# Attention, soft MoE and MLP in one kernel: another order of the attention turns, earlier preparation of two pairs, five more pooled chunks on GpSimd

## The chip, the cores and the metric

The kernel runs on one NeuronCore of one Trainium2 chip. The metric is the device time of one execution in microseconds (us). Before the change the median of 3 runs is 683.52 us (681.71 to 686.23).

## The reference, cut to what matters

Three layers run one after the other, all in float32:

```
k_p, v_p = mean over each 8 neighbouring rows of k, v      # 576 -> 72 rows
scores = q @ k_p.T / sqrt(64);  attn = softmax(scores);  x = attn @ v_p     # 8 batches x 8 heads
logits = x @ phi                                            # 4608 tokens, 32 slots
slot_in = softmax over tokens(logits).T @ x                 # dispatch
slot_out[e] = relu(slot_in[e] @ w1[e]) @ w2[e]              # 8 experts, w1 512x1024, w2 1024x512
y = softmax over slots(logits) @ slot_out                   # combine
out = (s * relu(y @ w_in)**2 + b) @ w_out                   # 512 -> 2048 -> 512
```

## The kernel before, in words

**The attention loop** (L709) is where the change lies. The 4608 tokens are 36 tiles of 128 queries. The 8 batches form four pairs (pr 0 to 3) of 9 tiles each; the first tile of a pair mixes the leftover 64 queries of both its batches. The loop has 38 turns, and it is a software pipeline written out by hand: turn t works on tile t in stage A, on tile t-2 in stage B, and so on. The stages and the engines that they use are:

- **A** (L348): four transposes of q on TensorE (L360) into a PSUM bank, one copy out by ScalarE (L362). After tiles 4 and 8 of a pair (counted from 0) it gives a q buffer back, so a load can be issued.
- **B**, tile t-2 (L372): scores on TensorE (L390) into one of two `sc` PSUM tiles; VectorE takes the row maximum `mx` (L397) and subtracts it into `S` (L399). There are two `S` buffers, so B of one tile writes the buffer that the tile two before it used.
- **C**, tile t-3 (L401): exp on ScalarE (L407), row sums `sm` and the reciprocal `rs` on VectorE (L408, L411), and the product P = S * rs on GpSimd (L428). This product is the last reader of the `S` buffer.
- **D**, tile t-5 (L436): five transposes of P on TensorE (L441, L442) into two banks, two copies by ScalarE (L447, L448).
- **E**, tile t-6 (L454): logits on TensorE (L464, L471), one copy by ScalarE. **F**, tile t-7 (L478): two transposes (L487) and a reduction by VectorE (L489). E and F do work in five of nine turns.
- **r** advances the running dispatch of a batch by one step (L540): small chains of TensorE, VectorE and ScalarE that end in the matmuls of L584 to L628. Its step with the transpose at L551 needs `md` from VectorE (L544).
- **p** advances the preparation of the next pair by one step (L637). A pair has six chunks, three of k and three of v. A chunk is pooled by three additions in SBUF (L258, L262, L263; the first `next` issues L258, the second the other two and gives the chunk's buffer back). In a plan, `kd2` means the next part of k chunk 2 on VectorE, `vg0` the next part of v chunk 0 on GpSimd, `K2` or `V2` the three transposes of that chunk on TensorE (L273) with their copies on ScalarE. After nine such steps come v_prep2, v_prep3 and v_prep1.

The order of the letters in LOOP (for turn t, the string t mod 9) or FIRST (turns 2 to 9) is the program order on every engine, and every engine works strictly in that order. PREP names the turns in which the preparations of pairs 1, 2 and 3 begin; PLAN1 is the plan of pair 1, PLAN2 that of pairs 2 and 3. The four-bank pool `w` holds the results of A, D, E, F and r in turn, so TensorE also waits where an earlier bank has not been read.

**Loads.** All loads are issued by SyncE (SP), in one fixed list: k, q and v of the pairs, then 32 expert weights of 1 MB, then the MLP's weights. There are 8 ring and 3 raw buffers of 1 MB; a load is issued when a buffer has been given back (`done`, L144). At the end of turn 32 the preparation's buffers become four more (`x`), and after the loop more come free as the attention's pools close (the X steps of TAIL).

**After the loop** come a tail of remaining steps (TAIL, L771), the expert layers in the order of their weights (L978), and the MLP, 576 x 3 matmuls of 512 columns at L1148. None of these is touched.

Of the kernel before, what the change touches and what calls it, by code (L numbers as in the profile page):

```python
# [25 lines left out]
CUT = 1  # L26

LOOP = (
# [9 lines left out]
)  # L38
FIRST = {
# [8 lines left out]
}  # L48
PREP = (5, 11, 19)
PLAN1 = "kd0 kd0|K0 kg1|kg1|K1 kd2 kd2 vg0|K2 vg0|vg2 vd1 V0 vg2 vd1||V1 V2"  # L50
PLAN2 = "kd2 kg0|kd2 kg0|kg1 K2|kg1 K0|vg0 vd2|vd2 vg0|V2 vg1 K1|V0 vg1|V1"
NRING, NRAW = 8, 3
LTB = 1
XR = (4, 2, 2, 2)
# [5 lines left out]
def kernel(  # L60
# [576 lines left out]
    def prep(pr):  # L637


        plan_ = PLAN1 if pr == 1 else PLAN2  # L640
        plan_ = [st.split() for st in plan_.split("|")]
        eng = {op[0] + op[2]: nc.gpsimd if op[1] == "g" else nc.vector for st in plan_ for op in st if len(op) == 3}
        ch = {(nm, c): pool_chunk(nm, pr, c, eng[f"{nm}{c}"]) for nm in "kv" for c in range(3)}
        for st in plan_:
            for op in st:
                if op[0] in "kv":
                    next(ch[op[0], int(op[2])], None)
                else:
                    kv_transpose(op[0].lower(), pr, int(op[1]))
            yield  # L650
        v_prep2(pr)
        yield
        v_prep3(pr)
        yield
        v_prep1(pr)
# [12 lines left out]
    def first_v():  # L668
        def pool_v(c, eng):
            for _ in pool_chunk("v", 0, c, eng):  # L670
                pass

        pool_v(0, nc.gpsimd)
        yield
        pool_v(1, nc.vector)
        pool_v(2, nc.gpsimd)
        yield
        kv_transpose("v", 0, 0)
        kv_transpose("v", 0, 1)
        yield  # L680
        kv_transpose("v", 0, 2)
        v_prep2(0)
        yield
        v_prep3(0)
        yield
        v_prep1(0)
# [15 lines left out]
    def advance(gens):  # L702
        for g in list(gens):
            if next(g, gens) is gens:
                gens.remove(g)
# [3 lines left out]
    for t in range(NT + 2):  # L709
        for op in (FIRST.get(t) or LOOP[t % 9]).split():  # L710
# [22 lines left out]
            elif op == "p":  # L733
                if t == 2 and not preps:
                    preps.append(first_v())
                if t in PREP:
                    preps.append(prep(PREP.index(t) + 1))
                advance(preps)
# [551 lines left out]
```

## Time and profile before

| what | value |
|---|---|
| median of 3 runs | 683.52 us |
| profiled execution, its own time | 682.68 us |
| span of its instructions | 680.9 us |
| busy: PE, DVE, ACT, POOL | 647.3, 470.2, 410.6, 288.3 us |
| mean granted clock of TensorE | 0.986 |

The profile names the engines PE (TensorE matmuls), PEld (its weight loads), DVE (VectorE), ACT (ScalarE), POOL (GpSimd) and SP (SyncE). L390 is line 390 of the kernel. Busy times overlap between engines. A granted clock of 1.00 is TensorE at its upper level of 2.4 GHz, 0.5 at its lower level of 1.2 GHz. Times within the trace count from the span's start; about 1.8 us of the execution lie outside the span.

### The profile page before, as it was taken

How to read it: one execution, taken by the hardware profiler on the slowest of the kernel's cores; microseconds unless marked ns; L12 is line 12 of the kernel's file. 1: busy time of each engine (PE TensorE's matmuls, PEld its weight loads, DVE VectorE, ACT ScalarE, POOL GpSimd, SP SyncE). 2: the span in 40 equal slices, each digit the busy share in tenths (PEclk: the TensorE clock that was granted, in tenths of full speed). 3: DMA queues.
4: the chain of work that ended last, by engine and by line, in shares of the span. 5: the costliest groups of instructions: out<-in, count | busy, mean ns of one | idle time of the engine just before them, and what ended most of it. 6: DMA issues, size and time to landing. Idle time of an engine off the chain costs nothing.

```text
span 680.9 us, 11539 instructions
## 1 busy us (share of the span) xinstructions
PE 647.3 (95%) x4474; PEld 523.7 (77%) x4474; DVE 470.2 (69%) x753; ACT 410.6 (60%) x684; POOL 288.3 (42%) x222
## 2 busy tenths in 40 slices
PE   7777999899899999999999999999999999999996
PEld 6666777678664678888888888888888888888885
DVE  4779678667775687887765978887557754566443
ACT  3564677566425578875666666666666666555551
POOL 3766567522211444462314433463233241999100
PEclk9897999999998999999999999999999999999999
DMA  8999476609699911110111110310100000222222
GB/s 291 403 341 280 175 247 250 231 20 317 256 333 375 389 63 63 62 28 36 63 63 33 46 46 1 124 62 4 60 0 1 1 0 1 93 93 93 93 93 92
DMA packets 41318, 88.88 MB, mean 131 GB/s; under 512 B 6960, under 2 KB 15152, under 8 KB 41264
## 3 DMA queue, kind: packets, MB, share of 16 engines
q1 hardware_dynamic: 41264, 88.16, 37.1%
q8 instruction: 35, 0.57, 0.4%
q14 instruction: 19, 0.16, 0.1%
HBM read 78.71 MB, written 9.44 MB: 129 GB/s over the span
## 4 chain that ended last, share of the span: by engine, by line
PE 80%; DVE 9%; DMA 5%; ACT 4%; issue 1%; SPq 1%; DVEq 0%; ACTq 0%
PE o L1148 58%; PE h L1088 5%; DMA ring<-in_moe_w_dram 3%; PE sc L390 3%; DVE sm L408 2%; DVE S L399 2%; DVE mx L397 1%; PE w L441 1%; PE w L607 1%; PE w L360 1%; DMA ring<-in_q_dram 1%; ACT S L407 1%; PE so_ps L998 1%; PE w L584 1%; PE w L250 1%
## 5 line engine op out<-in xcount | busy, mean ns | idle before, releaser
L1148 PE MATMUL o<-whi,gh 128*128 128x512 f32 x576 | 225.3, 391 | 0.6 <-DVE gh L1074 0.6
L1148 PE MATMUL o<-wlo,gh 128*128 128x512 f32 x576 | 224.9, 391 | 0.0
L1148 PE MATMUL o<-whi,gl 128*128 128x512 f32 x576 | 209.4, 392 | 0.0
L1116 DVE TENSOR_TENSOR gl<-r,gh 128x768 fp32r<-128x768 f32 (+1 forms) x97 | 105.8, 1092 | 115.2 <-ACT gh L1108 114.0
L1100 ACT ACTIVATE r<-h 128x768 f32<-128x768 f32 x94 | 76.5, 814 | 141.2 <-PE h L1088 139.2
L1148 PEld LDWEIGHTS o<-whi,gl 128*128 128x128 f32 x576 | 108.1, 188 | 23.2 <-DVE gl L1116 0.5
L1148 PEld LDWEIGHTS o<-whi,gh 128*128 128x128 f32 x576 | 108.1, 188 | 21.1 <-issue 1.0
L1148 PEld LDWEIGHTS o<-wlo,gh 128*128 128x128 f32 x576 | 108.2, 188 | 18.9
L842 POOL TENSOR_TENSOR fr<-fr,xp 128x512 f32<-128x512 f32 x28 | 45.3, 1616 | 176.9 <-ACT fr L841 156.5
L1161 DVE SCALAR_TENSOR_TENSOR part<-o,sb_t,part 128x512 f32<-128x512 f32 x144 | 96.9, 740 | 3.2 <-PE o L1148 3.1
L1101 ACT ACTIVATE r<-r 128x768 f32<-128x768 f32 x94 | 79.7, 848 | 3.0
L1108 ACT CAST gh<-r 128x768 fp32r<-128x768 f32 x94 | 78.6, 836 | 2.6
L428 POOL TENSOR_TENSOR P<-S,rs 128x576 f32<-128x576 f32 x32 | 37.3, 1166 | 69.9 <-DVE rs L411 36.5
L1259 POOL TENSOR_TENSOR part<-part,wsum 128x512 f32<-128x512 f32 x36 | 53.3, 1519 | 15.1 <-ACT wsum L1253 15.1
L1088 PE MATMUL h<-cT,S 128*128 128x384 f32 x192 | 49.5, 338 | 0.0
L1088 PEld LDWEIGHTS h<-cT,S 128*128 128x128 f32 x192 | 36.0, 188 | 8.1
L408 DVE TENSOR_REDUCE sm<-S 128x8 f32<-128x584 f32 x36 | 27.3, 758 | 21.1 <-ACT S L407 21.0
L390 PE MATMUL sc<-kb,qT 128*128 128x144 f32 x256 | 39.7, 301 | 0.2 <-ACT qT L362 0.2
L397 DVE TENSOR_REDUCE mx<-sc 128x8 f32<-128x576 f32 x36 | 26.4, 734 | 15.9 <-PE sc L390 13.2
L390 PEld LDWEIGHTS sc<-kb,qT 128*128 128x128 f32 x256 | 35.8, 203 | 0.7 <-ACT qT L362 0.5
L407 ACT ACTIVATE S<-S 128x576 f32<-128x576 f32 x36 | 24.7, 686 | 18.6 <-DVE S L399 17.5
L362 ACT COPY qT<-w 128x512 f32<-128x512 f32 x36 | 20.9, 584 | 21.3 <-PE w L360 20.4
(247 smaller groups left out, 901.1 us busy)
## 6 DMA issues: line engine op xcount, KB each, us to landing
x<-in_moe_w_dram SPq DMA_DIRECT2D x14, 1024.0 KB, 9.7
ring<-in_moe_w_dram SPq DMA_DIRECT2D x12, 1024.0 KB, 7.5
raw<-in_moe_w_in_dram SPq DMA_DIRECT2D x8, 1024.0 KB, 5.6
raw<-in_moe_w_out_dram SPq DMA_DIRECT2D x8, 1024.0 KB, 5.0
out_dram<-part SPq DMA_DIRECT2D x32, 256.0 KB, 2.6
ring<-in_q_dram SPq DMA_DIRECT2D x7, 1024.0 KB, 10.9
ring<-in_v_dram SPq DMA_DIRECT2D x9, 768.0 KB, 11.6
ring<-in_k_dram SPq DMA_DIRECT2D x7, 768.0 KB, 7.5
```

The costliest lines, as they stand in the source:

```text
L390: nc.tensor.matmul(out=sc[:, i // 2, 2 * KP * (i % 2):2 * KP * (i % 2) + 2 * KP], lhsT=qT[:, i, :], rhs=kb[:, H * bb + 4 * (j % 2) + i, :] ...
L408: nc.vector.tensor_reduce(out=sm, in_=S, axis=AX.X, op=ALU.add)
L428: nc.gpsimd.tensor_tensor(out=o, in0=S, in1=rb, op=ALU.mult)
L842: nc.gpsimd.tensor_tensor(out=fr, in0=fr, in1=xp, op=ALU.mult)
L1088: nc.tensor.matmul(out=h[x][:, 0:384] if i == 0 else h[:, x, 0:384], lhsT=Sw[:, f, :], rhs=cT(c, 384), start=True, stop=True)
L1100: nc.scalar.activation(out=r, in_=h[:, :, 0:384], func=ACTF.Relu)
L1101: nc.scalar.activation(out=r, in_=r, func=ACTF.Square)
L1108: nc.scalar.copy(out=gh_t[i], in_=r)
L1116: nc.vector.tensor_tensor(out=gl[:, x], in0=r[:, x], in1=gh[:, x].bitcast(F32), op=ALU.subtract)
L1148: nc.tensor.matmul(out=o_t[tt], lhsT=l[:, x, 128 * c:128 * c + 128], rhs=r, start=(fi == 0 and n == 0), stop=(fi == GROUPS[g] - 1 and n == 1),
L1161: nc.vector.scalar_tensor_tensor(out=p, in0=o_t[tt], scalar=sb_t[:, 0:1], in1=p, op0=ALU.mult, op1=ALU.add)
L1259: nc.gpsimd.tensor_tensor(out=p, in0=p, in1=wsum, op=ALU.add)
```

## The change

It writes the letters of every turn in another order, starts the preparations of pairs 1 and 2 one turn earlier, and rewrites both plans. In PLAN1, k chunk 0 moves from VectorE to GpSimd; k chunk 2 and v chunk 1 stay on VectorE. In PLAN2, which runs twice, k chunk 2 and v chunk 2 move to GpSimd, so that all six chunks are there. Some turns now have two p or none, and three or more r or none. The instructions are otherwise the same.

```
 LOOP = (
-    "F E C D r p B r A",
-    "F C E D r B p r A",
-    "F C D B E r A r p",
-    "F C E r D B A p r",
-    "F C E D B r A p r",
-    "F C E D p r A B r",
-    "F C E D r B A r p",
-    "F C E D r B A r p",
-    "F C E D B r A p r",
+    "B D C r E F A",
+    "p C B r F E D A r",
+    "F C r B r D E A p r",
+    "C E D B F A",
+    "p r F r C r B E p A r D",
+    "C F B r p E D A",
+    "F p B D r C E A",
+    "r C p p E r D B A F",
+    "r C r B r E r A D F",
 )
 FIRST = {
-    2: "F C E p B D r r w5 A",
-    3: "E F C r B p D r A",
-    4: "C E D F B A r r p",
-    5: "w3 D C r F B E p A r",
-    6: "C D q F B E A r r p",
-    7: "F C E B p A D r r",
-    8: "r F C B D A E p r",
-    9: "E F C B D r p r A",
+    2: "p B r r E D w5 F C A",
+    3: "D r p B p F C r A E",
+    4: "C B A p E F D",
+    5: "B p C r F A D E w3",
+    6: "C B r r p E F D A",
+    7: "E F C r B A D",
+    8: "B p A E r C D F",
+    9: "r F B r D r p r A C E r r r",
 }
-PREP = (5, 11, 19)
-PLAN1 = "kd0 kd0|K0 kg1|kg1|K1 kd2 kd2 vg0|K2 vg0|vg2 vd1 V0 vg2 vd1||V1 V2"
-PLAN2 = "kd2 kg0|kd2 kg0|kg1 K2|kg1 K0|vg0 vd2|vd2 vg0|V2 vg1 K1|V0 vg1|V1"
+PREP = (4, 10, 19)
+PLAN1 = "|kg0 kg0|kg1 kg1|kd2 vd1 K1 K0 kd2 vg0|vg0 K2|vg2 vd1 V0 vg2|V2||V1"
+PLAN2 = "kg2|kg2 kg0|vg2 kg0 kg1 K2||kg1|vg0 K0 vg2||vg0 vg1 K1|V0 V2 vg1|V1"
```

## Rows read from the trace of the kernel before

**Rows 1.** Busy us of each engine by stage (x instructions), granted clock, DMA share, GB/s.

```profile
15.00:65.00 50.00, 37.31 (x356) 31.25 (x356) 39.01 (x62) 27.19 (x63) 32.85 (x27) 0.86 1.05 360
65.00:148.00 83.00, 76.00 (x970) 60.66 (x969) 60.19 (x123) 57.20 (x144) 44.74 (x40) 1.00 0.55 192
148.00:178.00 30.00, 28.45 (x339) 23.37 (x337) 22.40 (x47) 17.70 (x43) 8.97 (x8) 1.00 0.59 211
198.00:235.00 37.00, 35.59 (x414) 17.31 (x410) 24.79 (x47) 18.98 (x42) 12.60 (x11) 0.95 1.03 384
```

**Rows 2.** Chain of waits, 175 to 300 us: start, us, what.

```profile
219.78 15.09 DMA ring<-in_moe_w_dram
```

**Rows 3.** SP's loads in order of time: start, us, queue line op, count.

```profile
152.53 2.85 SPq L139 DMA_DIRECT2D x<-in_moe_w_dram  x4
...
177.22 10.60 SPq L139 DMA_DIRECT2D x<-in_moe_w_dram  x6
195.71 0.88 SPq L139 DMA_DIRECT2D brief<-in_moe_w_dram  x2
```

**Rows 4.** Row maxima of tiles 9, 27, 28, 30 and 35 on VectorE: start, us.

```profile
57.80 0.71 DVE L397 TENSOR_REDUCE mx<-sc 128x8 f32<-128x576 f32 x1
...
144.29 0.71 DVE L397 TENSOR_REDUCE mx<-sc 128x8 f32<-128x576 f32 x1
...
148.10 0.76 DVE L397 TENSOR_REDUCE mx<-sc 128x8 f32<-128x576 f32 x1 [0.35 <-PE sc L390]
...
155.30 0.75 DVE L397 TENSOR_REDUCE mx<-sc 128x8 f32<-128x576 f32 x1
...
176.35 0.76 DVE L397 TENSOR_REDUCE mx<-sc 128x8 f32<-128x576 f32 x1 [1.61 <-PE sc L390]
```

**Rows 5.** Who waited for whom, 65 to 178 us: us, times, longest.

```profile
DVE sm L408 <- ACT S L407: 13.8, 19, 1.7
...
DVE mx L397 <- PE sc L390: 12.0, 9, 1.8
```

**Rows 6.** First additions of k chunk 2, pairs 1 and 2, on VectorE.

```profile
42.88 2.48 DVE L258 TENSOR_TENSOR raw<-raw 128x768 f32<-128x768 f32 x1
...
59.62 2.14 DVE L258 TENSOR_TENSOR raw<-raw 128x768 f32<-128x768 f32 x1
```

**Rows 7.** A chunk's three additions: ns min/median/max, first and last start.

```profile
L258 POOL TENSOR_TENSOR ring<-ring x10: 1806/1816/1921, 17.5 to 126.4; 128x768 f32<-128x768 f32 x10
...
L258 DVE TENSOR_TENSOR raw<-raw x5: 905/959/2476, 30.0 to 114.2; 128x768 f32<-128x768 f32 x5
...
L262 POOL TENSOR_TENSOR ring<-ring x10: 990/999/1592, 19.4 to 130.9; 128x384 f32<-128x384 f32 x10
...
L262 DVE TENSOR_TENSOR raw<-raw x5: 557/559/1217, 30.9 to 122.4; 128x384 f32<-128x384 f32 x5
...
L263 POOL TENSOR_TENSOR vp<-ring x7: 589/592/1294, 20.5 to 132.0; 128x192 f32<-128x192 f32 x7
...
L263 DVE TENSOR_TENSOR kp<-raw x3: 357/357/629, 31.5 to 65.4; 128x192 f32<-128x192 f32 x3
```

**Rows 8.** TensorE's wait for `md`, 15 to 65 us.

```profile
PE w L551 <- DVE md L544: 4.4, 1, 4.4
```

**Rows 9.** The scores of a tile in the chain of waits, before and after 65 us.

```profile
61.22 1.92 PE sc L390 x8
...
66.83 0.98 PE sc L390 x8
```

**Rows 10.** Busy us and granted clock, as in the first group, of one short stretch.

```profile
58.00:63.00 5.00, 3.24 (x15) 3.19 (x16) 4.68 (x7) 1.68 (x4) 3.10 (x3) 0.51 1.14 273
```

**Rows 11.** The product of stage C on GpSimd: ns min/median/max, first and last start.

```profile
L428 POOL TENSOR_TENSOR P<-S,rs x32: 1147/1149/1688, 26.8 to 180.5; 128x576 f32<-128x576 f32 x32
```

**Rows 12.** Load of a k chunk into a raw buffer, by SP and on the page.

```profile
40.54 0.51 SPq L139 DMA_DIRECT2D raw<-in_k_dram  x1
...
raw<-in_k_dram SPq DMA_DIRECT2D x5, 768.0 KB, 11.7
```

## The prediction

> **What bounds the kernel now.** I read the stages first: busy time by stage, granted clock and DMA share [rows 1]. The attention loop is the part up to 178 us. From 198 to 235 us the expert weights set the time: the DMA share is 1.03, and the chain of waits ends in one load of 15.09 us, from 219.78 to 234.87 [rows 1, 2]. After it stands the MLP, which the change doesn't touch. So the question has two halves: how much earlier the loop ends, and whether the weight loads follow it.
>
> They should. Six loads go out from 177.22 on, when the loop's last buffers come free, and two more at 195.71 [rows 3]. At 384 GB/s [rows 1] a load of 1.049 MB takes 2.7 us, so the 20 or so weights from 177.22 on (six x, two brief, and those that follow as buffers come back) fill about 55 us, nearly all of the 57.65 us to the last landing. A loop that ends d us earlier starts this train d earlier, and I carry d over whole.
>
> Then the pitch of the loop, taken from the row maxima of stage B [rows 4]. Tiles 9 to 27, with two preparations running beside them, take (144.29 - 57.80) / 18 = 4.80 us per turn. Tiles 27 to 35, almost without preparation, take (176.35 - 144.29) / 8 = 4.01. The quickest pair of turns, tiles 28 to 30, takes 3.60 each.
>
> What fills a turn changes on the way. Up to 65 us VectorE is the fuller engine (39.01 of 50 us), TensorE is busy for 37.31 only and at a granted clock of 0.86. From 65 to 148 us TensorE is busy for 76.00 of 83, VectorE for 60.19; from 148 to 178 it is 28.45 and 22.40 of 30 [rows 1]. So late in the loop TensorE is the nearest limit and only 7.0 and 1.55 us of visible gaps are left, while VectorE stands still because of the order: 13.8 us in front of `sm` for the exp, 12.0 in front of `mx` for the scores [rows 5]. In the old order C comes right after the B of the turn before, so subtraction, exp and sum follow each other with little between.
>
> **Part 1, five chunks from VectorE to GpSimd.** Alone, a chunk costs VectorE 0.96 + 0.56 + 0.36 = 1.88 us and GpSimd 1.82 + 1.00 + 0.59 = 3.41 [rows 7]. Beside a GpSimd addition the first of the three takes 2.14 or 2.48 instead of 0.96 [rows 6]; a chunk is then about 3.1 to 3.4. VectorE is thus relieved of 5 x 1.88 = 9.4 to 5 x 3.4 = 17 us; two of the five met such a neighbour plainly, so I take 12.5. GpSimd gets 5 x 3.41 = 17.1 us more, on top of 32.85 + 44.74 + 8.97 = 86.6 of the 163 us [rows 1]; 103.7 of 163 still fits.
>
> The place that gains most is around 60 us. There the dispatch's transpose waits 4.4 us for `md` [rows 8], since `md` stands on VectorE behind chunk work and the maxima of the same turns. After that gap the granted clock is 0.51 from 58 to 63 us [rows 10], the lower level of 1.2 GHz, and the scores of one tile take 1.92 us instead of 0.98 [rows 9]. Five us at 0.51 are 2.45 us lost on top of the gap. With k chunk 2 of pair 2 off VectorE, `md` straight after F and C, and its transpose at the end of that turn, I expect both to go. Late next there is v chunk 1 of pair 1, which stays on VectorE.
>
> Here a rule speaks against the change. The Trainium skill, GPSIMD Engine Reference, section Engine selection, says to put elementwise additions on VectorE, GpSimd being about twice as slow with two inputs. This trace has 3.41 against 1.88 us, 1.8 times; if each moved chunk cost its difference on the path, the sum would be 5 x 1.53 = 7.7 us up, 691.2. I don't take that, since GpSimd has room and VectorE's additions stand on the path around 43 and 60 us.
>
> **Part 2, the order of the letters.** In most turns B now precedes C and F. VectorE then has `mx` and the subtraction of one tile first, and the exp of the tile before runs meanwhile on ScalarE; the two waits of 25.8 us on VectorE [rows 5] shrink. What comes late next is TensorE itself, so the gain is bounded by its gaps. If only the visible gaps go, the pitch falls to 4.80 x 76.00 / 83 = 4.40 and to 4.01 x 28.45 / 30 = 3.80: 18 x 0.40 = 7.2 and 8 x 0.21 = 1.7 us. The other ends: nothing gained, 0, if TensorE's gaps only move to other places; or the turns with preparation come down to 4.01 and those without to 3.60, 18 x 0.79 + 8 x 0.41 = 17.5, since a busy TensorE can hide waits inside a modelled matmul. I take 7.2 and 1.7, near the end that the rows show directly. The lost clock and part of the 4.4 us gap lie inside these 18 turns, which is why I don't count part 1 again here.
>
> **Part 3, tiles 0 to 9, up to 57.80 us.** Gone from VectorE: k chunk 0 of pair 1, 1.9 us. Gained for VectorE: less waiting for exp. Against it, pooling now stands ahead of the product in turns 3 and 5: in turn 3 v chunk 2 of pair 0 (3.41 us) delays the product of tile 0 and with it the subtraction of tile 2, which needs that `S` buffer; v chunk 1 also precedes the maximum of tile 1 on VectorE. k chunk 2 and half of v chunk 1 now meet on VectorE in turn 8. Between -8 (TensorE is idle 50 - 37.31 = 12.7 us there, less the 4.4) and +4 (the turn 3 delay is never recovered) I take -3, because later turns have the slack to take the delay up.
>
> **Part 4, what GpSimd holds up.** An `S` buffer must be free one turn after its C. A turn of 4.8 us less `sm` and `rs` (0.96) and the product (1.15 [rows 11]) leaves 2.7 us for pooling ahead of the product. In turns 10, 13 and 22 the pooling ahead is 1.82 + 1.59 + 1.82 = 5.2 us, 2.5 too many. If all of it delayed VectorE and then TensorE, 7.5 us; if the product is late but VectorE has other work, 0. I take +1, near the lower end, since turns with little pooling follow each burst (12, 14, 23).
>
> **Part 5, loads.** The list and its order on SP stay; only the moments when buffers come back move. k chunk 0 of pair 1 comes back 1.5 us later from GpSimd, others earlier; up to 65 us the DMA share is 1.05 [rows 1], which covers that, and without the cover it costs 1.5 once. The first chunk of pair 2 is touched one turn earlier: its load goes out at 40.54 and by the median of 11.7 us lands at about 52.2 [rows 12], some 2 us before or after turn 10 needs it. A wait there would hold GpSimd's queue, with the product of tile 7 behind it; 0 to 2 us, inside the +1. v_prep1 of pair 3 moves from turn 30 to 32, so the four loads at 152.53 wait for it; 24.7 us lie between them and the next six [rows 3], and four loads need 11. Cost 0.
>
> **Sum.** -7.2 - 1.7 - 3 + 1 = -10.9 against the profiled execution of 682.68: 671.8. The median of runs is 0.8 above that execution, so I predict **672.5 us**.
>
> **Rivals.** (a) No gain to speak of: TensorE's work in its order is the limit already, the bank copies on ScalarE decide, and only the hole around 60 us closes. For it: 92% and 95% busy [rows 1]. Against it: 25.8 us of VectorE's waits. 4.4 + 2.45 = 6.9, half of which is lost again: 680. (b) Slower: the products of stage C become the bottleneck. GpSimd's queue delays the release of `S`, VectorE waits in front of the subtraction, `sc` stays full and TensorE waits in front of B. It decides once more than 2.7 us of pooling stand ahead of a product. Price: the three bursts 7.5, the four turns with 3.4 ahead (3, 5, 15, 24) 0.7 each, 2.8, so +10.3 with no gain beside it: 693.8. The rule on engine selection points to this case. Against it: GpSimd's share of 63% after the change. (c) The loop ends earlier but the weights don't: buffers before turn 33 would have to decide. Then 682.5. Against it: the train of loads starts at the loop's end [rows 3].
>
> **Chances.** Forecast 0.62, (a) 0.23, (b) 0.10, (c) 0.05. One per cent, 6.8 us, is about what a measurement of this kernel can tell from no change: faster means under 676.7, slower over 690.4. Of the forecast nearly nine tenths lie under 676.7; with a little of (a) that is 0.60. Slower is (b), 0.10. The rest, 0.30, is within 1%. The range: the low end takes the 17.5 of part 2 for half, 661; the high end takes in (a), (c) and a mild (b), 684.
>
> **What would show it.** Right: `mx` of tile 9 near 55 us, of tile 35 near 166; 18 turns of about 4.4 us; no half clock around 60 us; the wait of `sm` for the exp well under 13.8 us; the last weight landing near 224. Wrong: VectorE waiting in front of L399 for the product at L428; gaps of TensorE in front of L390 or D; a new stretch at the lower clock; or a loop end that moves while the last landing stays at 235.

## The result and the profile after

The changed kernel takes 665.78 us in the median (664.26 to 667.57), against 682.62 before (681.71 to 686.23) on the same chip: ratio 0.9745, 95% interval 0.9700 to 0.9789. That is 16.8 us faster, where 10.9 were forecast; it lies in the range. The profiled execution of the changed kernel took 667.57 us, with a span of 665.8. The span shrank by 15.1 us.

The row maxima of tiles 9, 27 and 35 in the changed kernel, to be held against [rows 4] (start, us):

```profile
55.49 0.74 DVE L397 TENSOR_REDUCE mx<-sc 128x8 f32<-128x576 f32 x1
...
132.01 0.75 DVE L397 TENSOR_REDUCE mx<-sc 128x8 f32<-128x576 f32 x1
...
160.66 0.70 DVE L397 TENSOR_REDUCE mx<-sc 128x8 f32<-128x576 f32 x1
```

Tile 9 comes 2.3 us earlier, tile 27 12.3, tile 35 15.7. The pitch fell from 4.80 to 76.52 / 18 = 4.25 us in the 18 turns with preparation and from 4.01 to 28.65 / 8 = 3.58 in the 8 after them.

What the engines did between these maxima (columns as in [rows 1]: busy us of PE, PEld, DVE, ACT, POOL, clock, DMA share, GB/s), first in the kernel before, then in the changed one:

```profile
57.80:144.29 86.49, 78.42 (x960) 63.33 (x961) 63.89 (x128) 57.26 (x144) 48.39 (x42) 0.96 0.62 208
144.29:176.35 32.06, 29.69 (x361) 24.22 (x358) 23.76 (x51) 20.23 (x50) 10.35 (x9) 1.00 0.55 198
```

```profile
55.49:132.01 76.52, 74.31 (x937) 62.25 (x937) 55.96 (x115) 55.74 (x140) 60.09 (x56) 0.98 0.76 248
132.01:160.66 28.65, 28.50 (x369) 23.98 (x369) 23.18 (x51) 20.20 (x50) 8.95 (x8) 1.00 0.63 222
```

TensorE's visible gaps shrank from 8.07 + 2.37 = 10.4 us to 2.21 + 0.15 = 2.4. That is 8.1 of the 13.4 us gained here. The other 5.3 came out of time in which TensorE counted as busy: 108.11 us became 102.81. Not all of this is waiting hidden in matmuls. The two windows hold 1306 matmuls instead of 1321, and 15 of them at the mean of 82 ns are about 1.2 us. In the 18 turns the granted clock also rose, from 0.96 to 0.98. In the 8 turns after them, at a clock of 1.00 on both sides, 361 matmuls took 29.69 us before and 369 take 28.50 now, so there busy time itself shrank. Over the whole span the same 4474 matmuls are busy for 641.2 us instead of 647.3, by the page (first line; the second is that of run 12 below, which has 644.5 us at a mean clock of 0.992 and is no faster than the kernel before, so a part of the 6.1 us can come without any gain in time):

```profile
PE 641.2 (96%) x4474; PEld 522.4 (78%) x4474; DVE 458.7 (69%) x738; ACT 410.7 (62%) x684; POOL 302.8 (45%) x237
...
PE 644.5 (95%) x4474; PEld 520.2 (76%) x4474; DVE 469.9 (69%) x753; ACT 409.9 (60%) x684; POOL 288.5 (42%) x222
```

The weight loads followed the loop. SP's loads in order of time (against [rows 3]), and the last landing in the chain of waits (against [rows 2]):

```profile
142.74 2.46 SPq L139 DMA_DIRECT2D x<-in_moe_w_dram  x4
...
163.32 9.99 SPq L139 DMA_DIRECT2D x<-in_moe_w_dram  x6
181.18 0.88 SPq L139 DMA_DIRECT2D brief<-in_moe_w_dram  x2
```

```profile
205.51 14.30 DMA ring<-in_moe_w_dram
```

The six loads go out 13.9 us earlier, the last weight lands at 219.81 instead of 234.87, 15.1 us earlier, and the span ends 15.1 us earlier. So 15.1 of the 15.7 us gained up to tile 35 arrive at the end.

Who waited for whom in the loop of the changed kernel (55 to 161 us: us, times, longest; against [rows 5]), and the hole around 60 us: TensorE's wait for `md` (against [rows 8]) and the stretch of [rows 10]:

```profile
DVE sm L408 <- ACT S L407: 11.7, 15, 1.8
...
DVE mx L397 <- PE sc L390: 5.5, 5, 1.5
DVE S L399 <- POOL P L428: 1.3, 2, 0.9
```

```profile
55.71 0.27 PE L551 MATMUL w<-ident,md 128*32 128x128 f32 x1 [0.84 <-DVE md L544]
```

```profile
58.00:63.00 5.00, 4.79 (x25) 4.50 (x26) 2.81 (x7) 2.65 (x7) 4.92 (x6) 0.66 1.18 242
```

The gap in front of L551 went from 4.4 us to 0.84, and TensorE works 4.79 us of these five instead of 3.24. The clock still has a stretch at its lower level there (mean 0.66 instead of 0.51). VectorE's wait for the scores halved; its wait for the exp, which I had named first, hardly fell. (Between the maxima of tiles 9 and 35 the two waits are 13.8 and 10.8 us before, 11.2 and 5.5 after.)

### The profile page after: what moved, and what is told of

Read it like the earlier page. It is cut to its first block, busy times and chain, and to the rows that moved or that the text cites. A ratio compares the mean times of both kernels' runs of the same rounds, so it can differ in the third digit from the quotient of the medians.

```text
span 665.8 us, 11549 instructions
## 1 busy us (share of the span) xinstructions
PE 641.2 (96%) x4474; PEld 522.4 (78%) x4474; DVE 458.7 (69%) x738; ACT 410.7 (62%) x684; POOL 302.8 (45%) x237
## 4 chain that ended last, share of the span: by engine, by line
PE 85%; DVE 5%; DMA 5%; issue 1%; POOL 1%; ACT 1%; SPq 1%; DVEq 0%; ACTq 0%; POOLq 0%
PE o L1148 58%; PE h L1088 5%; PE sc L390 4%; DMA ring<-in_moe_w_dram 2%; PE w L441 2%; PE w L360 2%; DMA ring<-in_v_dram 2%; PE w L607 1%; PE w L464 1%; DMA raw<-in_moe_w_dram 1%; PE w L584 1%; PE w L618 1%; PE l L987 1%; PE w L273 1%; PE so_ps L998 1%
## 5 line engine op out<-in xcount | busy, mean ns | idle before, releaser
L1148 PEld LDWEIGHTS o<-whi,gl 128*128 128x128 f32 x576 | 108.0, 188 | 23.3 <-DVE gl L1116 0.5
L1259 POOL TENSOR_TENSOR part<-part,wsum 128x512 f32<-128x512 f32 x36 | 53.3, 1520 | 15.1 <-ACT wsum L1253 15.1
L399 DVE TENSOR_TENSOR S<-sc,mx 128x576 f32<-128x576 f32 x36 | 27.3, 758 | 4.9 <-POOL P L428 1.6
## 6 DMA issues: line engine op xcount, KB each, us to landing
ring<-in_q_dram SPq DMA_DIRECT2D x7, 1024.0 KB, 12.5
```

Of the source, the lines that this page charges most:

```text
L399: nc.vector.tensor_tensor(out=S[:, :, :, 0:KP], in0=scv, in1=mx.unsqueeze(3).to_broadcast([128, 2, 4, KP]), op=ALU.subtract)
L1148: nc.tensor.matmul(out=o_t[tt], lhsT=l[:, x, 128 * c:128 * c + 128], rhs=r, start=(fi == 0 and n == 0), stop=(fi == GROUPS[g] - 1 and n == 1),
L1259: nc.gpsimd.tensor_tensor(out=p, in0=p, in1=wsum, op=ALU.add)
```

## The experiments

All ran beside the kernel before, whose medians were 682.1 to 682.4.

**1. The chunks alone** (before, with the new engines in the old plans):

```
-PLAN1 = "kd0 kd0|K0 kg1|kg1|...
+PLAN1 = "kg0 kg0|K0 kg1|kg1|...
-PLAN2 = "kd2 kg0|kd2 kg0|kg1 K2|kg1 K0|vg0 vd2|vd2 vg0|...
+PLAN2 = "kg2 kg0|kg2 kg0|kg1 K2|kg1 K0|vg0 vg2|vg2 vg0|...
```

> The kernel before in its old order and with its old starts of the preparations; only the five chunks go from VectorE to GpSimd. Theory A (the order of the letters gives most: it fills the waits of VectorE for exp and scores and the gaps of TensorE in every turn): 677 to 681, about -4, from the hole around 60 us alone; the 18 turns from tile 9 to 27 stay above 4.55 us. Theory B (the relief of VectorE gives most): 668 to 672, those turns at 4.3. Theory C (GpSimd's longer queue costs more than VectorE gains): 684 or more, with VectorE waiting for the product in front of the subtraction.

Measured: 679.05 us, ratio 0.9960 (0.9944 to 0.9976). Theory A's number, and its pitch, but not its place. The 18 turns take 83.86 us, 4.66 each, and the 8 after them are as before. The last two lines are from around 60 us:

```profile
58.00:141.86 83.86, 77.75 (x960) 63.27 (x961) 54.85 (x115) 57.32 (x144) 60.39 (x54) 0.96 0.64 213
141.86:173.91 32.05, 29.69 (x361) 24.22 (x358) 23.76 (x52) 20.23 (x50) 10.35 (x9) 1.00 0.55 198
...
58.00:63.00 5.00, 3.04 (x14) 3.00 (x15) 2.91 (x7) 1.68 (x4) 4.77 (x4) 0.55 1.13 290
...
59.96 0.40 PE L551 MATMUL w<-ident,md 128*32 128x128 f32 x1 [4.29 <-DVE md L544]
```

VectorE's busy time in these turns fell by 9.0 us (63.89 to 54.85), the turns by 2.6. The hole around 60 us stays: TensorE still waits 4.29 us for `md`, and the clock is 0.55. Up to tile 13 the maxima stand where they stood (79.17 us against 79.23); the gain comes between tiles 13 and 23 (122.76 against 125.19), and after that nothing is added.

**2. The order alone** (changed kernel, the five chunks back on VectorE):

```
-PLAN1 = "|kg0 kg0|...
+PLAN1 = "|kd0 kd0|...
-PLAN2 = "kg2|kg2 kg0|vg2 kg0 kg1 K2||kg1|vg0 K0 vg2|...
+PLAN2 = "kd2|kd2 kg0|vd2 kg0 kg1 K2||kg1|vg0 K0 vd2|...
```

> The changed kernel with the same five chunks back on VectorE; order, turns and starts of the preparations as changed. Theory A: 669 to 673, most of the gain stays. Theory B: 677 or more. If the parts only add up, the loss against the changed kernel equals the gain of the run with the chunks alone; if it is larger, the new order needs VectorE free.

Measured: 672.37 us, ratio 0.9864 (0.9847 to 0.9881), so most of the gain is the order's. Its pitch:

```profile
59.25:137.67 78.42, 73.25 (x937) 60.61 (x937) 67.07 (x127) 55.16 (x140) 49.70 (x43) 1.00 0.68 227
137.67:166.32 28.65, 28.49 (x369) 23.99 (x369) 23.18 (x51) 20.19 (x50) 8.95 (x8) 1.00 0.62 222
```

The stages of these four kernels side by side, each from its profiled execution:

| us | before | chunks alone | order alone | both |
|---|---|---|---|---|
| maximum of tile 9 | 57.80 | 58.00 | 59.25 | 55.49 |
| tiles 9 to 27 | 86.49 | 83.86 | 78.42 | 76.52 |
| tiles 27 to 35 | 32.06 | 32.05 | 28.65 | 28.65 |
| median of runs | 682.4 | 679.05 | 672.37 | 665.78 |

The last stage is the order's alone, to a hundredth. In the middle stage the order gives 8.1 us and the chunks about 2. The order alone also closes most of the hole around 60 us: TensorE's longest wait at L551 is 1.2 us there. The two alone give 3.3 and 10.0 us, together 13.3, against 16.8 for both; the difference of 3.5 is about the half width of the changed kernel's interval (0.0044 of 682 us, 3.0 us). By the three ratios it is 5.4 us, with about 3.4 either way from their intervals together. So that the parts help each other is likely, but not settled. If they do, it is before tile 9, where both together come 3.8 us earlier than the order alone. These are single executions: the maximum of tile 2, where the changed kernel and runs 2, 4, 7 and 8 don't differ yet, lies between 26.48 and 28.49 us in them.

**3. B to the front, nothing else** (in turns 10 to 37; one row shown):

```
-    "F E C D r p B r A",
+    "B F E C D r p r A",
```

> The kernel before, with B moved to the front of every turn from 10 on, nothing else. Theory A in its narrow form (it is B ahead of C that fills the waits): 675 to 679, and the wait of the row sum for the exp falls from 13.8 us to 7 or less between tiles 10 and 35. If the gain lies in other letters of the new order or in the chunks: 681 to 685, the wait falls without the turns getting shorter.

Measured: 693.24 us, ratio 1.0174 (1.0157 to 1.0192): slower, which no theory had. Its waits from 56 to 186 us, and its stages between the maxima of tiles 9, 27 and 35:

```profile
DVE mx L397 <- PE sc L390: 23.3, 18, 2.6
...
PE w L556 <- DVE md L553: 6.2, 4, 2.3
...
PEld w L360 <- ACT PT L447: 4.9, 6, 0.9
```

```profile
56.04:151.35 95.31, 81.14 (x950) 64.87 (x947) 64.89 (x127) 57.12 (x141) 51.60 (x44) 0.91 0.61 194
151.35:185.87 34.52, 31.13 (x334) 24.59 (x338) 23.88 (x52) 20.32 (x48) 8.35 (x8) 0.95 0.50 184
```

There is no row any more for VectorE's wait of `sm` for the exp, 13.8 us before; the wait that I had made my reason is wholly gone, and the kernel is 11 us slower. But VectorE's other wait, for the scores, grew from 10.8 to 23.3 us, so the two together hardly changed. From tile 9 to tile 35 the kernel takes 11.3 us more: TensorE's gaps grew by 7.1 us, and its busy time by 4.2, at a clock of 0.91 and 0.95 instead of 0.96 and 1.00. So part of the price was paid at the lower clock. TensorE now waits in front of A, where B used to stand between D and A in most rows, for a bank that ScalarE has yet to copy (in one row of nine A now follows D directly, in the others r, p or E stand between), and in front of the dispatch's matmul at L556, whose `md` on VectorE now comes after the new maximum and the row sum.

**4. Pair 2's first addition back to turn 11** (changed kernel):

```
-PREP = (4, 10, 19)
+PREP = (4, 11, 19)
 # pair 2 only:  "kg2|kg2 kg0|..."  ->  "kg2 kg2 kg0|..."
```

> The changed kernel, but the first addition of pair 2 (k chunk 2, 1.82 us on GpSimd) goes back from turn 10 to turn 11, where the second follows it. Theory A: the early start gives nothing by itself; without this addition ahead of the product of tile 7, which ends at 57.05, the subtraction of tile 9 comes up to 1.8 us sooner: 664 to 666. Theory D (the early start is what gains, by spreading GpSimd's load): 668 to 670.

Measured: 668.20 us (665.07 to 669.12), ratio 0.9797 (0.9769 to 0.9824). Nominally theory D, but the interval overlaps that of the changed kernel (0.9700 to 0.9789); by the ratios the early start of pair 2 is worth somewhere between nothing and some 7 us; not settled. Theory A's mechanism is there in the trace, in that the subtraction of tile 9 no longer waits for the product, but tile 9 doesn't come sooner: its maximum is at 57.60 us instead of 55.49, and that of tile 2, before anything differs, already at 28.49 instead of 27.34. From tile 9 to tile 35 this run takes 103.7 us and the changed kernel 105.2.

**5 and 6. D to the front too, then the dispatch's steps apart** (one row for all turns from 10 on, chunks and plans as before):

```
-    "F E C D r p B r A",
+    "B D F E C r p r A",     # run 5
+    "r B D F E C p A r",     # run 6, one r more in every ninth turn
```

> The kernel before with one order for all turns from 10 on: B D F E C r p r A. Against the run with B alone in front (693.2) this puts E and F between D and A; the two r stay close together with little between them. Theory E (with B in front, A stands right behind D, and its transposes wait until ScalarE has copied D's banks; B, which uses no bank of that pool, was the cover): 680 to 685, at least 8 us under that run. Theory F (the dispatch's steps, now without B between them, make TensorE wait for VectorE's md): 690 or more, little changes.

> As the run before, but the two r stand at the two ends of the turn: r B D F E C p A r (one r more in every ninth turn). Theory E alone: no change against that run, 680 to 685. Theory F alone: 682 or less while that run stays at 690. Both: that run at 683 to 687 and this one at 672 to 678, near the changed kernel's order with the chunks on VectorE (672.4), which would show that the gain of the new order is what stands between D, A and the dispatch's steps.

Measured: 706.34 us (ratio 1.0339, 1.0308 to 1.0369) and 704.93 (1.0342, 1.0312 to 1.0372). Theory E failed. Theory F's number held for run 5 (690 or more), but the steps apart, which it wanted at 682 or less, gained nothing that can be told. Waits of run 5 from 57 to 196 us:

```profile
ACT PT L447 <- PE w L441: 31.5, 23, 7.1
...
PE w L556 <- DVE md L553: 11.2, 5, 2.9
...
PEld w L441 <- POOL P L428: 9.5, 5, 6.1
```

TensorE's longest wait is the one in front of L556 for `md`. Beside it, with D ahead and C last, TensorE stands in front of D for the product, ScalarE stands in front of D's copies for TensorE, and the exp is queued behind those copies; the next product needs that exp. I read from this that D has to come late enough after the product, and that the exp must not be behind D's copies; no run separates the two from the wait at L556.

**7. All chunks on GpSimd** (changed kernel, `kd2` and `vd1` of PLAN1 to `kg2` and `vg1`):

> The changed kernel with the last two chunks of VectorE, k chunk 2 and v chunk 1 of pair 1, on GpSimd too. If VectorE's chunk work is still on the path around 43 to 52 us: 661 to 664. If GpSimd's queue is what holds products up there (the product of tile 7 ends at 57.05 and the subtraction of tile 9 waits 1.6 us for it): 668 to 671, with TensorE's gap in front of the pair's v transposes longer than 2.6 us and a longer stretch at the lower clock.

Measured: 668.88 us, ratio 0.9801 (0.9781 to 0.9820), about 3 us slower than run 8, which was on the same chip and has a ratio of 0.9759. (Run 8 has an edit of its own, which made no difference by itself; the interval of the changed kernel, 0.9700 to 0.9789, overlaps this run's a little.) As the second case said, GpSimd's queue holds products up around there. From 40 to 62 us:

```profile
DVE S L399 <- POOL P L428: 4.1, 2, 3.1
...
PE w L273 <- POOL vp L263: 3.5, 1, 3.5
```

TensorE's gap grew from 2.6 to 3.5 us, and the subtraction waits 4.1 us for the product, 1.2 in the changed kernel (0.86 of it at tile 9, not the 1.6 that the expectation gave). The maximum of tile 9 is at 57.16 us instead of 55.49, and from there to tile 35 it loses only 0.2 us more. So 2 more chunks on GpSimd, at this place, most likely cost, where the 5 gained.

**8. The transposes of v chunk 0 one turn later** (changed kernel):

```
-PLAN1 = "...|vg2 vd1 V0 vg2|V2||V1"
+PLAN1 = "...|vg2 vd1 vg2|V0 V2||V1"
```

> The changed kernel with the transposes of v chunk 0 of pair 1 moved from turn 10 to turn 11 (beside v chunk 2's). In the changed kernel TensorE stands 2.6 us at 46.5 us in front of them, waiting for GpSimd, and the clock is at its lower level from 58.2 to 61.6 us. If that wait is on the path: 662 to 664.5. If the maxima there are set by VectorE and GpSimd and not by TensorE: 665 to 667, no change.

Measured: 665.95 us, ratio 0.9759 (0.9741 to 0.9777): no change. TensorE's wait moved: the 2.6 us in front of L273 are gone, and the wait of D for the product grew from 1.0 to 3.0 us (40 to 62 us). The lower clock from 58 us on went, too:

```profile
PE w L441 <- POOL P L428: 3.0, 3, 1.9
```

```profile
58.00:63.00 5.00, 5.00 (x44) 4.75 (x42) 3.94 (x9) 4.11 (x12) 4.92 (x5) 1.00 1.15 271
```

The maximum of tile 9 comes at 54.57 us instead of 55.49, and its subtraction still waits for GpSimd's product, 1.2 us. So the wait that was taken away from TensorE is not what sets the time of the kernel.

**9, 10 and 11. One rule of place for all turns from 10 on** (chunks, plans and first turns as before):

```
-    "F E C D r p B r A",
+    "F E C B D r p r A",     # run 9, B behind C, each old row otherwise kept
+    "F E C B D r p A r",     # run 10
+    "C B r F E D p A r",     # run 11, one r more in every ninth turn
```

> The kernel before, with B moved from its late place to right behind C in every turn from 10 on, nothing else (in 7 of 9 turns of the new order B follows C, with D, E or F behind). The two r then have no B between them. Theory G (what the new order gains is that the scores are made early enough that VectorE goes from the row sum to the next maximum without waiting for TensorE, with C still ahead, so exp is not behind D's copies): 676 to 681; the wait of mx for the scores falls from 12 us to 6 or less; some of it is lost again at the dispatch's transposes. Theory H (no single rule of place gains; it is the places picked turn by turn, around the dispatch and the preparation): 683 or more.

> One order for all turns from 10 on, F E C B D r p A r: B behind C, and the second r behind A, so that p and A stand between the dispatch's steps. Chunks, plans and first turns as before. Theory G: 672 to 677. Theory H: 683 or more. If it gains over the run before while that one stands at 682, the dispatch's steps are what matters and not B.

> One order for all turns from 10 on, nearest to the new one: C B r F E D p A r (one r more in every ninth turn). Chunks, plans and first turns as before. Theory G: 670 to 676, that is, most of the 10 us that order and plans give without the chunks (672.4). Theory H: 683 or more, and then what the new order gains can't be given as one rule of place.

Measured: 691.85 (ratio 1.0159, 1.0140 to 1.0178), 692.25 (1.0150, 1.0133 to 1.0168) and 685.60 us (1.0059, 1.0041 to 1.0077). Theory H each time. Run 9, 57 to 183 us:

```profile
DVE sm L408 <- ACT S L407: 15.5, 14, 3.6
...
PE w L556 <- DVE md L553: 9.8, 6, 2.5
...
DVE mx L397 <- PE sc L390: 0.6, 1, 0.6
```

VectorE's wait for the scores, the other one of [rows 5], fell from 12.0 us to 0.6, and the kernel is 9.7 us slower. TensorE now waits 9.8 us for `md` in front of L556 (1.9 before), its longest wait. Run 10 has 10.7 us on the same wait, run 11 has 4.0 and only 3.5 us more time than before.

**12. The dispatch's steps at the new times, the old order otherwise** (before, only `r` moved):

```
-    "F C D B E r A r p",        # turns 11, 20, 29
-    "F C E r D B A p r",
-    "F C E D B r A p r",
+    "F C r D B r E A p r",
+    "F C E D B A p",
+    "r F r C r E D B A p r",
 ...
```

> The kernel before, with the letters A to F and p in their old order, chunks and plans as before; only the r of turns 10 to 37 are moved to the times of the new order: per ninth turn 1, 2, 3, 0, 4, 1, 1, 2 and 4 of them, so that the transpose of md (L551) stands at a turn's end and the matmul of L556 one or two turns later, at a turn's beginning. In the three runs with one rule of place TensorE waited longest in front of L556. Theory I (the times of the dispatch's steps are what gains, because there TensorE waits for a chain over VectorE and back): 673 to 678, the waits at L551 and L556 fall under 2 us. Theory J (the steps' times and the places of B, D and E gain only together, since early scores make VectorE late for md): 680 to 684, although those waits shrink.

Measured: 684.01 us, ratio 1.0031 (1.0013 to 1.0048). Theory J's number: no gain from this part alone. Waits from 57 to 179 us:

```profile
DVE mx L397 <- PE sc L390: 17.8, 13, 2.8
PE w L551 <- DVE md L544: 4.6, 2, 4.1
...
PE w L556 <- DVE md L553: 0.4, 2, 0.2
```

The wait at L556 is nearly gone, the one at L551 stays (4.1 us of it around 60 us), and the one in front of the scores grew from 12.0 to 17.8 us. In runs 3, 9 and 12 one wait was taken down by moving one letter or one kind of step, and each time another grew. In run 2, with the whole new order and plans but the old engines, the waits at L551 and for the scores are both small, and the wait for the exp nearly halved (59 to 167 us):

```profile
DVE sm L408 <- ACT S L407: 7.5, 11, 1.8
...
PE w L551 <- DVE md L544: 1.5, 3, 1.2
...
DVE mx L397 <- PE sc L390: 1.5, 2, 0.9
```

**What is shown, and what stays open.** Shown: the order and its plans alone give about 10 us, the five chunks alone 3; the pitch outside the preparation (tiles 27 to 35) is the order's alone; the weights follow the loop; and to remove one of VectorE's two waits alone doesn't shorten the pitch. Open: which turns of the new order carry the gain. Four uniform orders (runs 5, 6, 10 and 11), the new dispatch times alone, and B moved alone in two ways (runs 3 and 9) all fail to give it. No experiment exchanged single turns, and none separated the new order from the new times of the preparation's other steps. No run beat the changed kernel; run 8 equals it.

## Why the prediction was right or wrong, point by point

**The direction and the way to the end** were right. The loop's end moved, the train of weight loads moved with it (15.7 us at tile 35, 15.1 at the last landing), and rival (c) fell. The sum came out too small: by stages -9.97, -3.41 and -2.31 were measured where -7.2, -1.7 and -3 stood, and the +1 was not needed.

**Part 1, the chunks.** The sign was right, the place wrong. I wrote that the place that gains most is around 60 us. With the chunks alone the hole there is as deep as before (run 1: 4.29 us of wait, clock 0.55), and 2.4 us come later, between tiles 13 and 23; it is the order that takes the wait in front of L551 down (run 2: 1.2 us). What stands ahead of `md` on VectorE in run 1 is v chunk 1 of pair 1, which I had named as next. The relief of VectorE was set at 12.5 us and is 10.8 by the pages of the kernel before and of run 1 (470.2 and 459.4 us busy); one of the two stretched additions that I took it from, that of pair 1, belongs to a chunk that stays on VectorE. The factor in the engine-selection rule of the Trainium skill (GPSIMD Engine Reference, Engine selection), about twice as slow on GpSimd, agrees with 3.41 us for a chunk against 1.88. The 7.7 us that I had worked out against the change did not come: moved alone, the chunks gained 3.3. Run 7 shows a place where the slower engine most likely costs: two more chunks ahead of a product, about 3 us.

**Part 2, the order.** The step that failed in size is "only the visible gaps go": 7.2 and 1.7 us were set, 9.97 and 3.41 measured. As gaps the term was nearly right, 8.9 set and 8.1 measured; the other 5.3 us came out of time that the profile counts as busy. About 1.2 of these are the 15 matmuls that the windows hold fewer, and by an estimate 0.9 are the shorter stretch at the lower clock (from 58 to 68 us, by halves, the clock was 0.51 and 0.81 before and is 0.66 and 1.00 now); the rest is busy time that shrank, as in the last 8 turns. I had named that end (17.5 us) and leaned to the other.

The reason that I gave failed in part. I wrote that in most turns B now precedes C and F; of the nine rows of the new loop B precedes C in two and both in one, and in seven B follows C. The two waits do shrink with the order alone, from 24.6 to 9.0 us between tiles 9 and 35 (run 2). The wait for the exp stays at 11.2 of 13.8 in the changed kernel, since the chunks push it up: alone they raise it to 17.0, most likely because VectorE has less other work to fill the time with. But that the waits' shrinking is the cause of the gain isn't shown. Run 3 removed the wait for the exp and run 9 the one for the scores, and both were slower. So the forecast's direction rests on the bound by TensorE's gaps, and that the number came as near as it did is partly luck. I take it that the gaps of TensorE close when D, A, the scores and the dispatch's steps all stand far enough behind what they need; I had not worked that out, and no run shows it by itself.

**Part 3, tiles 0 to 9.** -3 set, -2.3 measured, in single executions that differ by 2 us at tile 2 among themselves. The delay in turn 3 came, but GpSimd's v chunk 2, which I had named first, is not what ends last. The delay is there at the maximum of tile 1 already, which starts at 22.49 us instead of 18.96: VectorE has v chunk 1 ahead of it and waits 4.21 us for that chunk's load. The product of tile 0 then starts 0.54 us after GpSimd is done with v chunk 2: it needs VectorE's row sum and reciprocal, and the row sum waits for an exp that stands behind the copies of v on ScalarE. In the changed kernel, VectorE, ScalarE and GpSimd:

```profile
19.68 0.96 DVE L258 TENSOR_TENSOR ring<-ring 128x768 f32<-128x768 f32 x1 [4.21 <-DMA ring<-in_v_dram]
20.67 1.23 DVE L262 TENSOR_TENSOR ring<-ring 128x384 f32<-128x384 f32 x1
...
22.49 0.74 DVE L397 TENSOR_REDUCE mx<-sc 128x8 f32<-128x576 f32 x1
...
25.37 0.76 DVE L408 TENSOR_REDUCE sm<-S 128x8 f32<-128x584 f32 x1 [1.34 <-ACT S L407]
```

```profile
23.29 1.34 ACT L292 ACTIVATE vt<-w 64x192 f32<-64x192 f32 x4 [5.53 <-PE w L273]
24.65 0.68 ACT L407 ACTIVATE S<-S 128x576 f32<-128x576 f32 x1
```

```profile
25.38 0.59 POOL L263 TENSOR_TENSOR vp<-ring 128x192 f32<-128x192 f32 x1
26.52 1.15 POOL L428 TENSOR_TENSOR Pm<-S,rs 128x576 f32<-128x576 f32 x1 [0.54 <-ACT S L407]
```

The subtraction of tile 2 follows its own maximum and waits for no product. A stretch at the lower clock that is longer than before comes with this delay, one of the signs of being wrong that I had listed (20 to 25 us, before and after):

```profile
20.00:25.00 5.00, 2.06 (x13) 1.73 (x13) 4.84 (x7) 2.45 (x6) 4.92 (x4) 0.89 1.06 382
```

```profile
20.00:25.00 5.00, 2.60 (x12) 2.42 (x13) 3.92 (x5) 1.64 (x5) 4.84 (x4) 0.56 1.06 380
```

The delay, 3.1 us at tile 2, was taken up again by tile 9, as set.

**Part 4, GpSimd's bursts.** +1 set; VectorE waits 1.3 us for products in two turns of the whole loop from 55 us on. Turn 12, which I had counted among those with little pooling, has 3.4 us ahead of its product too (the plan step of turn 11). The burst of turn 10 is one of the two: the products of tiles 7 and 8 leave together from 55.90, and the subtraction of tile 9 waits 0.86:

```profile
54.14 1.81 POOL L258 TENSOR_TENSOR raw<-raw 128x768 f32<-128x768 f32 x1
55.90 2.26 POOL L428 TENSOR_TENSOR P<-S,rs 128x576 f32<-128x576 f32 x2
```

```profile
57.09 0.76 DVE L399 TENSOR_TENSOR S<-sc,mx 128x576 f32<-128x576 f32 x1 [0.86 <-POOL P L428]
```

Rival (b) was the right mechanism at about an eighth of its price; run 7 feeds it and gets more of it. **Part 5, loads:** no addition on GpSimd from turn 4 on waited for a load, and the four loads after turn 32 went out at 142.74, 9.8 us earlier rather than later. So far cost 0, as set; the wait of 4.21 us for the load of v chunk 1 (part 3), now that its additions stand ahead of a maximum, was not in this part.

**Rival (a)**, that TensorE is the limit already, was nearer than its 0.23 in one sense: after the change TensorE is 97% busy between tiles 9 and 27 and 99% after. But the 92% of before was no floor.

## What to carry to other kernels

In a pipeline written out by hand a wait in the profile is a symptom of the whole order: removing it by moving one letter can make another wait grow by as much or more, so judge an order by the pitch of a whole period and by the gaps of the fullest engine. The wait of an engine that is not the limit says little by itself: VectorE's wait for the exp rose with the chunks and fell with the order, and both gained. A gap of TensorE can cost more than its length, where the granted clock is lower after it, as in the hole around 60 us (0.51) and in run 3 (0.91 over the 18 turns). Elementwise work may go to the slower engine where that engine has room; ahead of its work on the path it can cost.

## What the runs showed of the hardware that was not expected

Additions in SBUF on VectorE and GpSimd that run beside each other can stretch on both sides; the prediction had counted VectorE's side only. In the changed kernel GpSimd's second addition took 1.76 us (0.99 alone, [rows 7]) while VectorE ran its own additions at 19.68 and 20.67 us (the lines of part 3):

```profile
19.73 1.76 POOL L262 TENSOR_TENSOR ring<-ring 128x384 f32<-128x384 f32 x1
```

Of these three the first on VectorE took 0.96 us, as alone, and its second 1.23 (0.56 alone). Each of the two that stretched began while an addition of the other engine was running, and took about as much longer as that one still had to go (0.91 and 0.82 us by these lines; 0.77 and 0.67 longer).
